# Attention on pairs of 64-row matmuls: three terms for z by z, and sums of each row half in banks of their own

## The chip, the core and the metric

The kernel runs on one core of a Trainium2 chip. The metric is device time in microseconds (us) of one execution. The kernel before was timed in three runs, with a median of 1893.45 us (1893.43 to 1894.5). A profile is one further execution, recorded by the hardware. Engines are named as in the profile: PE is TensorE (PEld its weight loads), DVE VectorE, ACT ScalarE, POOL GpSimd, SP SyncE. A PSUM bank holds 512 float32 columns on 128 partitions (rows); there are eight, `banks[:, 0]` to `banks[:, 7]`.

## The reference

Two stages, with no softmax between them:

```python
# u, v: (4, 3008, 256)   z: (4, 3008, 64)
scores = (1.0 / S) * np.matmul(z, z.transpose(0, 2, 1))   # S = 3008
attn = np.maximum(scores, 0.0) ** 2
out = np.matmul(attn, v)
x = (u * out).reshape(12032, 256)
gate = 1.0 / (1.0 + np.exp(-(x @ w_gate)))                # w_gate, w_val: 256 x 1536
val = x @ w_val
result = gate * val @ w_out                               # w_out: 1536 x 256
```

The change concerns the first stage: the scores (z by z, over 64 elements) and their product with v (over 3008 keys).

## The kernel before

**Precision.** Each float32 operand is split into a high part, rounded by ACT or DVE to the type fp32r, and a low part, the remainder, so a product is a sum of terms: high by high, low by high, high by low.

**Work.** The four batches b are cut into six chunks c of 512 queries (the last has 448) and twelve blocks i of 256 keys, in two halves j of 128 keys each. A step is one (b, c, i): 288 steps, in the order of the list `steps` (line 144). Since the scores are symmetric, a block that an earlier chunk has computed is turned by DVE (`turn`, line 415), stored to DRAM and loaded back later as one of this chunk's steps (`load_back`, line 451): such a step computes no scores (`back`, line 147). One step of each of the first five chunks, the last in its chunk, computes half of its queries (`half`), except in the very first chunk, whose scores are all computed.

**One step.** `pe_scores` (line 334) writes 128 keys by up to 512 queries for each j, into one of two pairs of banks (0 and 1, or 2 and 3) in turn. z has 64 elements a token, and the arrays that hold its parts carry them twice: on rows 0 to 63 and again on 64 to 127. The query tile (`z_query`) holds the high part on the upper 64 rows and the low part on the lower, so one 128-row matmul gives the key part against both query parts: two matmuls for each j, four a step. ACT takes the scores through relu and square into `r` (lines 356, 357), rounds them into `ah` (line 372; on some steps DVE does, line 370), and DVE takes the remainder `al` (line 377). `pe_pv` (line 481) then multiplies by v: for each j and each half d of v's 256 columns, high v by high a, low v by high a, high v by low a. That is twelve 128-row matmuls a step (ten where the last key block is stacked), summed over the chunk's twelve steps in a pair of banks (4 and 5, or 6 and 7, by turns from chunk to chunk), one bank for each d. At a chunk's end `keep` (line 507) copies the two banks to SBUF by one ACT instruction, and a step later sends them to DRAM.

**Order.** The program is written out by hand, in the order in which each engine runs it. In round g of the main loop (line 851) PE gets the scores of step g + 2 and, last, the product of step g. In between stand the loads of later steps, the store and turn of earlier ones, the square, rounding and remainder of step g + 2, jobs entered by round in the tables `before` and `after` (splitting weights, loading z and v of the next batch), and in the first round of a chunk `keep` of the chunk before, behind the rounding. In `after` stand the two DMAs of `z_both` (line 272), which fill the query tile of each chunk ten rounds ahead on SP's queue.

**The end of attention.** The products of the last two steps are issued between the first matmuls of the second stage, by the generator `others` (line 935), in the parts that `pe_pv` yields. That stage uses banks 0 to 3 for its products and 4 to 7 for its sums, and is not part of the change.

Of the kernel before, what the change touches and what calls it, by code (L numbers as in the profile page):

```python
# [9 lines left out]
F32R = mybir.dt.float32r  # L10
# [3 lines left out]
AF = mybir.ActivationFunctionType  # L14
ALU = mybir.AluOpType
# [11 lines left out]
def kernel(  # L27
# [10 lines left out]
    nc = tc.nc  # L38
    P = 128
    B, S, D = u.shape  # L40
# [3 lines left out]
    CH = 512  # L44
    NCH = (S + CH - 1) // CH
    NPAIR = (S + 255) // 256
    NB = D // P
# [21 lines left out]
    v_a, z_a, zq_a, r_a, ah_a, al_a, al2_a, turned_a, raw_a, zt_a, keep_a, w_a, spare_a = map(area, sizes)  # L69
# [9 lines left out]
    banks = ps.tile([P, 8, CH], F32, name="banks")  # L79

    def part(a, kb, cols, dt=F32):

        ap = a[:, int(kb * KB) : int(kb * KB) + cols]
        return ap if dt is F32 else ap.bitcast(dt)

    def f32(ap):
        return ap.bitcast(F32)

    def moving(ap):

        return ap.rearrange("p (t n) -> p n t", t=2)

    def product(ap):

        return ap.rearrange("p (n t) -> p t n", t=2)

    def products(ap):
        return ap.rearrange("p j (n t) -> p j t n", t=2)

    def by_half(ap):  # L100
        return ap.rearrange("p (t n) -> p t n", t=2)

    def by_halves(ap):
        return ap.rearrange("p j (t n) -> p j t n", t=2)
# [39 lines left out]
    steps = [(b, c, i) for b in range(B) for c in range(NCH) for i in order(b, c)]  # L144
    number = {s: g for g, s in enumerate(steps)}
# [93 lines left out]
    z_raw, z_t = {}, {}  # L239

    def z_place(b, p):
        n = (b * NCH + p) % 7
        return part(z_a, 2 * n, CH, F32R), part(z_a, 14 + 2 * n, CH, F32R)

    def z_query(b, p):
        return part(zq_a, 2 * ((b * NCH + p) % 2), CH, F32R)

    def load_z(b, p):
        t = part(w_a, 2 * p, CH) if b == 0 else part(raw_a, 6, CH)
        t = t.rearrange("p (T d) -> p T d", d=32)  # L250
# [17 lines left out]
    def z_low(b, p):  # L268
        hi, lo = z_place(b, p)
        nc.vector.tensor_tensor(lo, z_t[b, p], f32(hi), op=ALU.subtract)  # L270

    def z_both(b, p):
        (hi, lo), q = z_place(b, p), z_query(b, p)
        nc.sync.dma_start(f32(q[0:64]), f32(hi[0:64]))
        nc.sync.dma_start(f32(q[64:128]), f32(lo[64:128]))

# [47 lines left out]
    def keys_of(i, ap, j):  # L326
        if i == NPAIR - 1:
            return ap[:, j * P : j * P + P]
        return ap.rearrange("p (n j) -> p j n", j=2)[:, j]

    sc_t = {}
    counts = {"sc": 0, "turned": 0}

    def pe_scores(s):
        b, c, i = s
        if back(s):
            return
        n = chunk(c)
        k = 2 * (counts["sc"] % 2)
        counts["sc"] += 1  # L340
        sc = banks[:, k : k + 2]
        kh, kl = z_place(b, i // 2)
        q0 = CH // 2 if half(s) else 0
        q = moving(z_query(b, c)[:, q0:n])
        for j in range(2):
            o = (i % 2) * 256
            h, l = (keys_of(i, ap[:, o : o + 256], j) for ap in (kh, kl))
            nc.tensor.matmul(sc[:, j, 0 : n - q0], h, q, start=True, stop=False)  # L348
            nc.tensor.matmul(sc[:, j, 0 : n - q0], l, q, start=False, stop=True)  # L349
        sc_t[s] = sc  # L350

    def square(s):
# [98 lines left out]
    def load_back(s):  # L451
        b, c, i = s
        r = r_of(s)
        if half(s):
            nc.sync.dma_start(r[:, :, 0 : CH // 2], half_t[b, c].rearrange("(p j) q -> p j q", j=2))
        if back(s):
            n, d = chunk(c), shared_t[b, i // 2, c]
            if late(b, i // 2):
                for g in range(4):
                    t = as_stored(i)[32 * g : 32 * g + 32].rearrange("p (I B q) -> p I B q", I=2, q=64)  # L460
                    q0 = 256 * (i % 2) + 64 * g
                    for I in range(2):
                        src = d[I].rearrange("p g j q -> p (g j) q")[:, :, q0 : q0 + 64]
                        nc.gpsimd.dma_start(t[:, I], src)
            else:
                rows = d[256 * (i % 2) : 256 * (i % 2) + 256].rearrange("(p j) q -> p j q", j=2)
                nc.sync.dma_start(r[:, :, 0:n], rows[:, :, 0:n])
# [6 lines left out]
            for k in range(2):  # L474
                nc.vector.transpose(out=dst[:, k], in_=src[:, k])

    def acc_of(b, c):
        k = 4 + 2 * ((b * NCH + c) % 2)
        return banks[:, k : k + 2]

    def pe_pv(s):

        b, c, i = s
        n, k = chunk(c), number[s] % NPAIR
        acc = acc_of(b, c)
        (ah, al), (vh, vl) = a_of(s), v_place(b, i)
        for j in range(2):
            stacked = i == NPAIR - 1 and j == 1
            stop = k == NPAIR - 1 and j == 1
            for d in range(NB):  # L490
                ds = slice(d * P, (d + 1) * P)
                o = acc[:, d, 0:n]
                nc.tensor.matmul(o, vh[:, j, ds], moving(ah[:, j, 0:n]), start=(k == 0 and j == 0), stop=False)  # L493
                if not stacked:
                    nc.tensor.matmul(o, vl[:, j, ds], moving(ah[:, j, 0:n]), start=False, stop=False)  # L495
                if d == 0:
                    yield
            for d in range(NB):
                ds = slice(d * P, (d + 1) * P)
                nc.tensor.matmul(acc[:, d, 0:n], vh[:, j, ds], moving(al[:, j, 0:n]), start=False, stop=stop)  # L500
            yield

# [2 lines left out]
    def keep(b, c, store):  # L507
        n, t0 = chunk(c), b * S + c * CH
        C = b * NCH + c
        if C == B * NCH - 1:  # L510
            t = part(turned_a, 8, 2 * CH)
        else:
            t = part(keep_a, 4 * ((C + 1) % 2) if b < B - 1 else 0, 2 * CH)
        t = t.rearrange("p (h q) -> p h q", h=NB)
        if store:
            nc.sync.dma_start(sums[:, :, t0 : t0 + n], t[:, :, 0:n])
        else:
            nc.scalar.activation(by_halves(t[:, :, 0:n]), products(acc_of(b, c)[:, :, 0:n]), AF.Copy)

# [214 lines left out]
    with tc.manual_schedule():  # L736
# [3 lines left out]
        before, after = {}, {}  # L740

        def at(when, g, f, *args):
            when.setdefault(g, []).append((f, args))
# [6 lines left out]
        for b in range(1, B):  # L750
# [12 lines left out]
            for i in range(NPAIR):  # L763
# [1 line left out]
                at(after, g - 1, load_v, b, i)  # L765
                at(before, g + 2, v_high, b, i)
                at(before, g + 2, v_low, b, i)
        for b in range(B):
            for p in range(NCH):
                if (b, p) != (0, 0):  # L770
                    at(after, b * per + NPAIR * p - 10, z_both, b, p)
        starts = [24, 31, *range(84, 127, 7), *range(156, 199, 7), 246, 261]
        for n, g in enumerate(starts):
            job = Narrow(n)
# [28 lines left out]

        def keep_warm(n):
            for _ in range(n):
                nc.tensor.matmul(banks[:, 7], idle[:, 0:P], idle, start=True, stop=True)

        load_z(0, 0)
        zero = part(r_a, 12, P)
# [6 lines left out]
        load_z(0, 3)  # L816
        turn_z(0, 0)
        z_high(0, 0)
        q = z_query(0, 0)
        nc.scalar.activation(q[0:64], z_t[0, 0][0:64], AF.Copy)  # L820
        z_low(0, 0)
        nc.vector.tensor_copy(q[64:128], f32(z_place(0, 0)[1][64:128]))  # L822
        load_z(0, 4)
        load_v(0, 2)
        keep_warm(11)
# [25 lines left out]
        for g, (b, c, i) in enumerate(steps[:-2]):  # L851
            nxt = steps[g + 2]
            k = g % NPAIR
            early = g < NPAIR
            if g < 3:
                for _ in pe_pv(steps[g]):
                    pass
            pe_scores(nxt)
            if early:
                if k + 2 < NPAIR:  # L860
                    v_low(0, k + 2)
                if k + 5 < NPAIR:
                    load_v(0, k + 5)
                if k in (2, 3, 5):
                    z_low(0, {2: 3, 3: 4, 5: 5}[k])
                if k in (0, 2, 4):
                    turn_z(0, k // 2 + 3)
            for s in steps[g + 5 : g + 8]:
                if number[s] - g == (7 if comes_late(s) else 5):
                    load_back(s)  # L870
            if k == 1 and g > 1:
                keep(*steps[g - 2][:2], True)
            store_turned(steps[g])
            turn(steps[g + 1])
            if not back(nxt):
                square(nxt)
            round_up(nxt)
            rest(nxt)
            if g + 4 < len(steps):
                turn_late(steps[g + 4])  # L880
            run(before, g)
            if early and k + 3 < NPAIR:
                v_high(0, k + 3)
            if early and k in (1, 2, 4):
                z_high(0, {1: 3, 2: 4, 4: 5}[k])
            if k == 0 and g:
                keep(*steps[g - 1][:2], False)
            run(after, g)
            if g >= 3:
                for _ in pe_pv(steps[g]):  # L890
                    pass
# [154 lines left out]
```

## Time and profile before

| what | value |
|---|---|
| median of three timed runs | 1893.45 us (1893.43 to 1894.5) |
| profiled execution, first to last instruction (span) | 1891.7 us |
| PE busy, matmuls | 1880.6 us (99%), 8890 |
| PEld busy, weight loads | 1656.5 us (88%), 8890 |
| DVE busy | 1538.2 us (81%) |
| ACT busy | 1138.8 us (60%) |
| POOL busy | 920.3 us (49%) |

The page gives of the profiled execution the span alone; the 1.75 us between it and the median lie around the first and last instruction or between executions. Matmuls are pipelined and their ends are modelled: a matmul of 512 columns is shown with 379 ns although the next one starts earlier, so strides are read from starts, not from durations. A weight load is shown with some 190 ns beside the matmul before it. In the stretches of rows further down, the columns give each engine's busy time, in brackets its instructions, then the granted clock of PE as a share and the mean busy share of the 16 DMA engines.

### The profile page before, as it was taken

Reading aid. Unit: us, or ns where it says so; the run is one execution under the profiler, and the core shown is the slowest. Engines: PE = TensorE matmul, PEld = TensorE weight load, DVE = VectorE, ACT = ScalarE, POOL = GpSimd, SP = SyncE. Lnnn points to the kernel's source line nnn. Section 1 sums busy time; section 2 is a strip of 40 time slices with the busy share of each in tenths; the row PEclk is TensorE's granted clock in tenths of the full one; section 3 lists DMA queues with packets and bytes.
Section 4 is the critical chain, followed back from the end, with each engine's and each line's share of the span. In section 5 each row is a group of like instructions: output and inputs, shape, how many; then the busy total and the mean of one; then the engine's idle time right before and its main releaser. Section 6 shows DMA issues by size and latency. Waiting matters only on the chain.

```text
span 1891.7 us, 26376 instructions
## 1 busy us (share of the span) xinstructions
PE 1880.6 (99%) x8890; PEld 1656.5 (88%) x8890; DVE 1538.2 (81%) x1957; ACT 1138.8 (60%) x1497; POOL 920.3 (49%) x853
## 2 busy tenths in 40 slices
PE   9999999999999999999999999999999999999998
PEld 7888988889888988889888888888888888888898
DVE  7797688888888786767879787888879797888876
ACT  8886788867887787774444453444444444445443
POOL 4334201230013200003777776877777787778675
PEclk9999999999999999999999999999999999999999
DMA  7789688997799888886542524243342525242331
GB/s 203 182 222 247 184 177 228 276 306 182 177 266 285 249 196 216 220 253 211 173 117 68 145 81 104 84 120 99 90 113 86 126 84 121 81 118 80 99 101 37
DMA packets 552295, 302.98 MB, mean 160 GB/s; under 512 B 490080, under 2 KB 506912, under 8 KB 552160
## 3 DMA queue, kind: packets, MB, share of 16 engines
q1 hardware_dynamic: 534928, 254.51, 51.0%
q0 software_dynamic: 14832, 46.38, 7.8%
q8 instruction: 70, 1.15, 0.3%
q10 hardware_dynamic: 2400, 0.41, 0.1%
q14 instruction: 65, 0.53, 0.1%
HBM read 192.02 MB, written 103.15 MB: 156 GB/s over the span
## 4 chain that ended last, share of the span: by engine, by line
PE 92%; DVE 2%; ACT 2%; DMA 2%; issue 1%; SPq 1%; DVEq 0%; POOL 0%; POOLq 0%
PE banks L693 19%; PE banks L633 12%; PE banks L635 11%; PE banks L634 11%; PE banks L500 11%; PE banks L493 11%; PE banks L495 10%; PE banks L349 3%; PE banks L348 3%; DVE al L377 1%; PE banks L724 1%; DMA shared<-spare 1%; ACT r L356 1%; ACT ah L372 1%; ACT r L357 1%
## 5 line engine op out<-in xcount | busy, mean ns | idle before, releaser
L666 POOL TENSOR_TENSOR keep<-keep,spare 128x512 f32<-128x512 f32 (+1 forms) x284 | 386.6, 1372 | 240.8 <-DVE keep L658 240.8
L377 DVE TENSOR_TENSOR al<-r,ah 128x1024 fp32r<-128x1024 f32 (+1 forms) x287 | 341.0, 1191 | 157.5 <-ACT ah L372 152.0
L493 PE MATMUL banks<-ah,v 128*128 128x512 f32 (+1 forms) x1152 | 428.2, 375 | 0.8 <-DVE ah L385 0.3
L495 PE MATMUL banks<-ah,v 128*128 128x512 f32 (+1 forms) x1104 | 413.5, 375 | 0.0
L500 PE MATMUL banks<-al,v 128*128 128x512 f32 (+1 forms) x1152 | 339.2, 376 | 2.9 <-DVE al L377 2.0
L372 ACT ACTIVATE ah<-r 128x1024 fp32r<-128x1024 f32 (+1 forms) x252 | 256.7, 1034 | 57.1 <-DMA r<-shared 27.4
L670 ACT ACTIVATE h<-keep 128x512 fp32r<-128x512 f32 (+1 forms) x144 | 89.7, 623 | 283.2 <-POOL keep L666 280.1
L658 DVE TENSOR_TENSOR zt<-banks,zt 128x512 f32<-128x512 f32 (+1 forms) x288 | 193.7, 672 | 68.0 <-ACT zt L652 55.5
L500 PEld LDWEIGHTS banks<-al,v 128*128 128x128 f32 x1152 | 216.3, 189 | 33.6 <-DVE al L377 8.3
L493 PEld LDWEIGHTS banks<-ah,v 128*128 128x128 f32 x1152 | 217.7, 189 | 27.4 <-ACT ah L372 1.1
L495 PEld LDWEIGHTS banks<-ah,v 128*128 128x128 f32 x1104 | 208.7, 189 | 24.4
L356 ACT ACTIVATE r<-banks 128x1024 f32<-128x1024 f32 (+2 forms) x169 | 163.1, 965 | 100.1 <-PE banks L349 99.1
L676 POOL TENSOR_TENSOR h<-keep,h 128x512 fp32r<-128x512 f32 (+1 forms) x143 | 187.4, 1311 | 55.7 <-ACT h L670 55.7
L662 ACT ACTIVATE spare<-spare 128x512 f32<-128x512 f32 (+1 forms) x288 | 174.3, 618 | 66.0 <-DVE spare L658 64.5
L658 DVE TENSOR_TENSOR spare<-banks,zt 128x512 f32<-128x512 f32 (+1 forms) x288 | 188.1, 673 | 22.3 <-PE banks L635 21.6
L357 ACT ACTIVATE r<-r 128x1024 f32<-128x1024 f32 (+2 forms) x169 | 170.0, 1006 | 5.4
L652 ACT ACTIVATE zt<-banks 128x512 f32<-128x512 f32 (+1 forms) x144 | 84.0, 583 | 145.3 <-PE banks L635 139.3
L231 POOL DMA_DIRECT2D w_gv<-w x24 | 13.4, 560 | 312.5 <-ACT w L225 299.6
L633 PE MATMUL banks<-z,v 128*128 128x512 f32 x378 | 144.3, 382 | 0.0
L635 PE MATMUL banks<-z,v 128*128 128x512 f32 x378 | 143.3, 379 | 0.0
L348 PE MATMUL banks<-zq,z 128*128 128x512 f32 (+2 forms) x340 | 123.7, 366 | 0.8 <-DVE zq L822 0.8
L670 ACT ACTIVATE v<-keep 128x512 fp32r<-128x512 f32 (+1 forms) x144 | 89.0, 618 | 58.3 <-POOL keep L666 49.2
(161 smaller groups left out, 3930.7 us busy)
## 6 DMA issues: line engine op xcount, KB each, us to landing
v<-w_gv SPq DMA_DIRECT2D x75, 896.0 KB, 4.7
r<-shared SPq DMA_DIRECT2D x72, 512.0 KB, 4.8
shared<-turned SPq DMA_DIRECT2D x236, 128.0 KB, 3.1
r<-shared SPq DMA_DIRECT2D x38, 448.0 KB, 6.0
shared<-spare SPq DMA_DIRECT2D x128, 128.0 KB, 3.4
out_dram<-turned SPq DMA_DIRECT2D x176, 64.0 KB, 2.0
w_gv<-w POOLq DMA_DIRECT2D x24, 448.0 KB, 4.9
sums<-keep SPq DMA_DIRECT2D x20, 512.0 KB, 3.9
```

The costliest lines, as they stand in the source:

```text
L357: nc.scalar.activation(r[:, :, q0:n], r[:, :, q0:n], AF.Square)
L372: nc.scalar.activation(ah[:, :, 0:n], r[:, :, 0:n], AF.Copy)
L377: nc.vector.tensor_tensor(al[:, :, 0:n], r[:, :, 0:n], f32(ah[:, :, 0:n]), op=ALU.subtract)
L493: nc.tensor.matmul(o, vh[:, j, ds], moving(ah[:, j, 0:n]), start=(k == 0 and j == 0), stop=False)
L495: nc.tensor.matmul(o, vl[:, j, ds], moving(ah[:, j, 0:n]), start=False, stop=False)
L500: nc.tensor.matmul(acc[:, d, 0:n], vh[:, j, ds], moving(al[:, j, 0:n]), start=False, stop=stop)
L633: nc.tensor.matmul(o, wt[:, 0, w], xh, start=True, stop=False)
L634: nc.tensor.matmul(o, wt[:, 0, w], xl, start=False, stop=False)
L635: nc.tensor.matmul(o, wt[:, 1, w], xh, start=False, stop=True)
L658: nc.vector.tensor_tensor(to[:, 0:m], bank(J, value, name), s_t[other][:, 0:m], op=ALU.add)
L666: (nc.vector if J == last else nc.gpsimd).tensor_tensor(y, y, g, op=ALU.mult)
L693: nc.tensor.matmul(o, wt[:, half_w, f, ds], moving(ap[:, 0:m]), start=start, stop=stop)
```

## The change

Scores are computed by matmuls on 64 rows: half j = 0 of the keys on rows 0 to 63, j = 1 on rows 64 to 127, each into its own bank, with three terms (high by high, low by high, high by low) and the terms of the two halves taking turns. The query tile goes, with the DMAs and copies that filled it: queries are read from the arrays of z. In the product with v every 128-row matmul becomes two of 64 rows, r = 0 and 1, one after the other in the program; each d now has a pair of banks, one for each r. The order within a step is d, then j, then the three passes. The last two steps of attention keep 128-row matmuls (`whole`), all into the bank of r = 0. `keep` adds the two banks of each d: ACT copies the first, DVE adds the second. It now stands ahead of the stores, the turn and the squares of its round.

Banks 2 to 7 form three pairs that rotate: chunk number C has its sums of d in pair 2C + d, modulo 3. Scores of even steps go to banks 0 and 1, of odd steps to the third pair, which the chunk does not use.

```diff
@@ z_query, and z_both: gone @@
@@ pe_scores @@
+    def rows_half(r):
+        return slice(64 * r, 64 * r + 64)
+    def pair_of_banks(n):
+        k = 2 + 2 * (n % 3)
+        return banks[:, k : k + 2]
+    def scores_of(s):
+        g = number[s] - 2
+        if g % 2:
+            return pair_of_banks(2 * (max(g, 0) // NPAIR) + 2)
+        return banks[:, 0:2]
...
-        k = 2 * (counts["sc"] % 2)
-        counts["sc"] += 1
-        sc = banks[:, k : k + 2]
-        kh, kl = z_place(b, i // 2)
+        sc = scores_of(s)
         q0 = CH // 2 if half(s) else 0
-        q = moving(z_query(b, c)[:, q0:n])
-        for j in range(2):
-            o = (i % 2) * 256
-            h, l = (keys_of(i, ap[:, o : o + 256], j) for ap in (kh, kl))
-            nc.tensor.matmul(sc[:, j, 0 : n - q0], h, q, start=True, stop=False)
-            nc.tensor.matmul(sc[:, j, 0 : n - q0], l, q, start=False, stop=True)
+        o = (i % 2) * 256
+        keys = [ap[:, o : o + 256] for ap in z_place(b, i // 2)]
+        queries = [moving(ap[:, q0:n]) for ap in z_place(b, c)]
+        for x, (kx, qx) in enumerate(((0, 0), (1, 0), (0, 1))):
+            for j in range(2):
+                r = rows_half(j)
+                nc.tensor.matmul(
+                    sc[:, j, 0 : n - q0], keys_of(i, keys[kx], j)[r], queries[qx][r], start=x == 0, stop=x == 2
+                )
@@ pe_pv @@
-    def acc_of(b, c):
-        k = 4 + 2 * ((b * NCH + c) % 2)
-        return banks[:, k : k + 2]
+    def acc_of(b, c, d):
+        return pair_of_banks(2 * (b * NCH + c) + d)
...
+        whole = number[s] >= len(steps) - 2
+        for d in range(NB):
+            acc = acc_of(b, c, d)
+            ds = slice(d * P, (d + 1) * P)
+            for j in range(2):
+                passes = [(vh, ah), (vl, ah), (vh, al)]
+                if i == NPAIR - 1 and j == 1:
+                    del passes[1]
+                for x, (vx, ax) in enumerate(passes):
+                    start = k == 0 and j == 0 and x == 0
+                    ends = j == 1 and x == len(passes) - 1
+                    halves = [(0, slice(0, P))] if whole else [(r, rows_half(r)) for r in range(2)]
+                    for r, p in halves:
+                        stop = ends and number[s] in ((len(steps) - 1, len(steps) - 3)[r], number[s] - k + NPAIR - 1)
+                        nc.tensor.matmul(acc[:, r, 0:n], vx[p, j, ds], moving(ax[p, j, 0:n]), start=start, stop=stop)
+                yield
@@ keep @@
-            nc.scalar.activation(by_halves(t[:, :, 0:n]), products(acc_of(b, c)[:, :, 0:n]), AF.Copy)
+        for d in range(NB):
+            to, acc = by_half(t[:, d, 0:n]), acc_of(b, c, d)
+            nc.scalar.activation(to, product(acc[:, 0, 0:n]), AF.Copy)
+            nc.vector.tensor_tensor(to, product(acc[:, 1, 0:n]), to, op=ALU.add)
@@ main loop, round g @@
+            if k == 0 and g:
+                keep(*steps[g - 1][:2], False)
             if k == 1 and g > 1:
                 keep(*steps[g - 2][:2], True)
             store_turned(steps[g])
...
-            if k == 0 and g:
-                keep(*steps[g - 1][:2], False)
             run(after, g)
```

Beside these, the matmuls that keep PE's clock up before the first scores write bank 5 and not 7.

## Rows read from the trace of the kernel before

**Rows 1.** The page's totals: busy us, share of the span, instructions.
```profile
span 1891.7 us, 26376 instructions
...
PE 1880.6 (99%) x8890; PEld 1656.5 (88%) x8890; DVE 1538.2 (81%) x1957; ACT 1138.8 (60%) x1497; POOL 920.3 (49%) x853
```

**Rows 2.** The chain of waits that ended last, by engine.
```profile
PE 92%; DVE 2%; ACT 2%; DMA 2%; issue 1%; SPq 1%; DVEq 0%; POOL 0%; POOLq 0%
```

**Rows 3.** Timeline of PE at a chunk's end: start us, us, engine, line, operation.
```profile
265.18 0.38 PE L348 MATMUL banks<-zq,z 128*128 128x512 f32 x1
...
272.08 0.38 PE L348 MATMUL banks<-zq,z 128*128 128x512 f32 x1
```

**Rows 4.** The same in a chunk of 448 queries.
```profile
207.00 0.35 PE L348 MATMUL banks<-zq,z 128*128 128x448 f32 x1
...
208.51 0.54 PE L500 MATMUL banks<-al,v 128*128 128x448 f32 x2
```

**Rows 5.** Groups of PE's matmuls by line and shape: count, busy us, mean ns, idle before.
```profile
L493 PE MATMUL banks<-ah,v 128*128 128x512 f32 x960 | 361.2, 380 | 0.8 <-DVE ah L385 0.3 <-DVE ah L370 0.2 <-ACT ah L372 0.2
L495 PE MATMUL banks<-ah,v 128*128 128x512 f32 x920 | 348.7, 379 | 0.0
...
L348 PE MATMUL banks<-zq,z 128*128 128x512 f32 x282 | 107.0, 379 | 0.8 <-DVE zq L822 0.8
...
L493 PE MATMUL banks<-ah,v 128*128 128x448 f32 x192 | 67.0, 352 | 0.0
L495 PE MATMUL banks<-ah,v 128*128 128x448 f32 x184 | 64.9, 352 | 0.0
...
L348 PE MATMUL banks<-zq,z 128*128 128x256 f32 x38 | 9.7, 277 | 0.0
L348 PE MATMUL banks<-zq,z 128*128 128x448 f32 x20 | 7.1, 353 | 0.0
```

**Rows 6.** Timeline of PE and its loads where a step has 256 queries.
```profile
259.10 0.27 PE L348 MATMUL banks<-zq,z 128*128 128x256 f32 x1
259.10 0.19 PEld L349 LDWEIGHTS banks<-zq,z 128*128 128x128 f32 x1
...
259.22 0.20 PEld L348 LDWEIGHTS banks<-zq,z 128*128 128x128 f32 x1
...
259.34 0.20 PEld L349 LDWEIGHTS banks<-zq,z 128*128 128x128 f32 x1
...
259.56 0.38 PE L493 MATMUL banks<-ah,v 128*128 128x512 f32 x1
```

**Rows 7.** Timeline in the first steps, where PE had waited: two loads, two matmuls.
```profile
10.80 0.30 PEld L500 LDWEIGHTS banks<-al,v 128*128 128x128 f32 x2 [0.48 <-DVE al L390]
10.80 0.70 PE L500 MATMUL banks<-al,v 128*128 128x512 f32 x2
```

**Rows 8.** Timeline of PE at the kernel's end, nine matmuls of 256 columns.
```profile
1880.91 1.17 PE L724 MATMUL banks<-al,v 128*128 128x256 f32 x9
```

**Rows 9.** The page's groups of instructions: reads of a bank by DVE and ACT.
```profile
L658 DVE TENSOR_TENSOR zt<-banks,zt 128x512 f32<-128x512 f32 (+1 forms) x288 | 193.7, 672 | 68.0 <-ACT zt L652 55.5
...
L652 ACT ACTIVATE zt<-banks 128x512 f32<-128x512 f32 (+1 forms) x144 | 84.0, 583 | 145.3 <-PE banks L635 139.3
```

**Rows 10.** Timeline of ACT and DVE at the chunk's end of rows 3.
```profile
271.85 1.06 ACT L372 ACTIVATE ah<-r 128x1024 fp32r<-128x1024 f32 x1
...
272.94 1.23 DVE L377 TENSOR_TENSOR al<-r,ah 128x1024 fp32r<-128x1024 f32 x1 [0.71 <-ACT ah L372]
```

**Rows 11.** Timeline of ACT before the first scores are squared.
```profile
6.71 0.63 ACT L301 ACTIVATE v<-turned 128x512 fp32r<-128x512 f32 x1 [0.85 <-DMA turned<-in_v_dram]
```

**Rows 12.** Stretches of chunks (b, c) = (0, 0), (1, 4) and (2, 2), columns as told above.
```profile
12.40:55.60 43.20, 42.76 (x194) 36.34 (x193) 33.97 (x44) 37.82 (x45) 21.66 (x40) 1.00 0.66 190
...
384.00:415.30 31.30, 30.55 (x142) 25.95 (x141) 26.15 (x35) 22.51 (x25) 12.56 (x21) 1.00 0.96 299
...
526.80:563.60 36.80, 36.80 (x174) 32.47 (x173) 31.95 (x38) 32.67 (x35) 7.33 (x12) 1.00 1.02 261
```

More of the change, by code (lines that the diff above doesn't have):

```diff
@@ L243, in z_place @@
         return part(z_a, 2 * n, CH, F32R), part(z_a, 14 + 2 * n, CH, F32R)
-    def z_query(b, p):
-        return part(zq_a, 2 * ((b * NCH + p) % 2), CH, F32R)
     def load_z(b, p):
@@ L270, in z_low @@
         nc.vector.tensor_tensor(lo, z_t[b, p], f32(hi), op=ALU.subtract)
[L272 to L275, printed above, removed]
     v_raw = {}
@@ L331 @@
     sc_t = {}
-    counts = {"sc": 0, "turned": 0}
+    counts = {"turned": 0}
+    def rows_half(r):
[8 more added lines that the diff above has]
+        return banks[:, 0:2]
     def pe_scores(s):
@@ L484, in pe_pv @@
         n, k = chunk(c), number[s] % NPAIR
-        acc = acc_of(b, c)
         (ah, al), (vh, vl) = a_of(s), v_place(b, i)
[L487 to L501, printed above, removed]
+        whole = number[s] >= len(steps) - 2
[14 more added lines that the diff above has]
+                yield
     sums = dram.tile([P, NB, N], F32, name="sums")
@@ L516, in keep @@
             nc.sync.dma_start(sums[:, :, t0 : t0 + n], t[:, :, 0:n])
-        else:
-            nc.scalar.activation(by_halves(t[:, :, 0:n]), products(acc_of(b, c)[:, :, 0:n]), AF.Copy)
+            return
+        for d in range(NB):
+            to, acc = by_half(t[:, d, 0:n]), acc_of(b, c, d)
+            nc.scalar.activation(to, product(acc[:, 0, 0:n]), AF.Copy)
+            nc.vector.tensor_tensor(to, product(acc[:, 1, 0:n]), to, op=ALU.add)
     groups = [(t0, min(CH, (N - t0) // 2)) for t0 in range(0, N, 2 * CH)]
@@ L767 @@
                 at(before, g + 2, v_low, b, i)
[L768 to L771, printed above, removed]
         starts = [24, 31, *range(84, 127, 7), *range(156, 199, 7), 246, 261]
@@ L805, in keep_warm @@
             for _ in range(n):
-                nc.tensor.matmul(banks[:, 7], idle[:, 0:P], idle, start=True, stop=True)
+                nc.tensor.matmul(banks[:, 5], idle[:, 0:P], idle, start=True, stop=True)
         load_z(0, 0)
@@ L818 @@
         z_high(0, 0)
-        q = z_query(0, 0)
-        nc.scalar.activation(q[0:64], z_t[0, 0][0:64], AF.Copy)
         z_low(0, 0)
-        nc.vector.tensor_copy(q[64:128], f32(z_place(0, 0)[1][64:128]))
         load_z(0, 4)
```

## The prediction

> **What bounds the kernel now.** I read the page's totals first: PE is busy for 1880.6 us of a span of 1891.7 [rows 1]. A busy PE need not be PE at its peak, so next I read the chain of waits: it runs through PE for 92% [rows 2]. Last I looked at where matmuls start. In attention, 32 matmuls of 512 columns lie between 265.18 and 272.08 us, one every 6.90/32 = 0.2156 us [rows 3]; at 448 columns eight take 1.51 us, 0.189 each [rows 4]. The time goes with the columns and nothing lies between. So PE is bound by columns, and what counts is how many slots of 0.2156 us there are. The load of each matmul's weights runs beside the matmul before it, hidden.
>
> **What changes in slots.** Differences are worked out in the profiled execution (span 1891.7 us) and put on the median of the timed runs, 1893.45, which lies 1.75 us above that span.
>
> Scores. Line 348 has 282 matmuls of 512 columns, 20 of 448 and 38 of 256, two for each step, so 141, 10 and 19 steps compute scores; line 349 has as many again [rows 5]. Each of these steps has four 128-row matmuls: for j = 0 and 1, high keys and low keys, each against high and low queries stacked on 128 rows. After, it has three terms for each j on 64 rows, j = 0 on rows 0 to 63 and j = 1 on 64 to 127: six matmuls, three slots if two of them run side by side. Four of 256 columns now take 0.46 us, 0.115 each [rows 6]. One slot less a step is 141 x 0.2156 + 10 x 0.189 + 19 x 0.115 = 30.4 + 1.9 + 2.2 = 34.5 us.
>
> Product with v. Lines 493, 495 and 500 have 960 + 920 + 960 = 2840 matmuls of 512 columns and 192 + 184 + 192 = 568 of 448 (line 500 counts as line 493) [rows 5]. The last two steps (24 of the latter) stay on 128 rows. The other 3384 become pairs: each half has the same columns, so a pair costs one slot if the halves run together. The trace has no 64-row matmul, so its cost is open between two ends. Side by side: 0. One behind the other: 2840 x 0.2156 + 544 x 0.189 = 715 us more. I take 0: the halves share neither rows nor a bank, and in the rows PE is a stream of columns through rows.
>
> Weight loads. Each half has a load of its own, of 128 columns as before. Two loads on end take 0.30 us [rows 7] where one takes 0.19 [rows 6], so the second starts 0.11 after the first; their two matmuls span 0.70, of which 0.38 is the second one [rows 7] and 0.2156 a stride, which leaves 0.104 for the same load. I take 0.108 a load. Two of them make 0.216 us, almost exactly a slot of 512 columns: were loads to follow one another, they would just hide there, and not under 448 or 256 columns. If besides a load waits until the matmul before it has started, the rows of 256 columns give the step: loads 0.12 apart, each starting with a matmul, 0.117 a matmul for the keys ((259.56 - 259.10 - 0.11)/3) [rows 6], and (1.17 - 0.27)/8 = 0.1125 for nine with other weights [rows 8]. Halves that load beside each other show none of this: 0, the end that I take, as each half has rows of its own.
>
> The Trainium skill bears on this twice (TensorE: Matmul & The Clock Gate). "LDWEIGHTS (loading the stationary operand)" says that a load's time goes by its columns, so that one of few rows costs as much as a full one; by that rule halving the rows halves no load, which speaks against the change, and rivals 1 and 2 are what it would do here. Part 3, "The mechanism" and "What overlaps and what doesn't", says that loads overlap matmuls in flight when their row groups differ, and that tiles start about 4 ns apart; if each of the 3894 pairs paid those 4 ns, an estimate from the page is 15.6 us more and the sum would be -4 us. No row of before shows either.
>
> **The handover at a chunk's end.** Before, two pairs of banks for sums alternate, and ACT copies one at leisure (line 518, behind the rounding). After, three pairs rotate. The d = 1 sums of a new chunk go into the pair that held the old chunk's d = 0 sums, so PE waits for an ACT copy of 128x512 out of a bank (583 ns in line 652) and then a DVE add out of a bank (672 ns in line 658) [rows 9]. Their place in the queues decides. Take the boundary at 272.08, where the old chunk's matmuls end [rows 3]. ACT is at line 372 from 271.85 for 1.06 us; the copy follows at 272.9 and ends at 273.5. DVE starts the remainder, line 377, at 272.94 for 1.23 us, to 274.17 [rows 10]; the add ends at 274.85. PE does three slots of scores (0.65) and six of d = 0 (1.29) and is ready for d = 1 at 272.08 + 1.94 = 274.02. It stands for about 0.85 us. This needs two computed steps in a row, as at the boundaries into chunks 0, 1 and 2 of a batch, 11 of 23; where the second is loaded back, the rounding is over earlier and I count up to 0.1. That is 11 x 0.85 + 1 = 10 us more. The ends are 0 (the add in time everywhere) and 23 x 1.7 = 39 (every boundary, each with twice the delay). Behind the waiting copy on ACT stand the second copy and the next squares; behind the add on DVE the next turn and remainder, which PE's own stop gives time.
>
> **What is taken away or moved.** 46 copies of z into the query tile leave SP's queue: a relief, counted 0. The two small ones at the start go; PE waits 0.8 us for the second [rows 5], but ACT stands until 6.71 for v's transfer anyway [rows 11], so I take 0, with -0.8 as the end. Since ACT and not PE paces the first steps, the slots of some four steps there are saved in vain: 1 us more. The low part of a is wanted at the third slot of a step and not the fifth, 0.43 us earlier: by rows 10 it is there at 274.17, for a step that starts at 272.08 + 0.65 + 2.59 + 0.65 = 275.97, so 0; up to 1 us a chunk if that cover goes, within the 39 above.
>
> **What the DMAs give back.** In chunks 2 to 4 of batches 1 and 2 the DMA engines are busy for 0.96 to 1.02 of the time, and PE stands 31.30 - 30.55 = 0.75 us in one of these six stages [rows 12]. There, and in the same three of batch 3, the change saves 18 slots a batch, 11.6 us in all. I take a third of it, 4 us, as lost to late loads; the ends are 0 and 11.6. In the first chunk ACT is busy for 37.8 of 43.2 us [rows 12], which stays under the 40.6 that are left after twelve slots: 0.
>
> **Sum.** -34.5 + 0 + 10 + 1 + 4 = -19.5 us: 1874 us, 1.0% faster. With the ends of the last terms this case reaches from 1862 to 1886, and beyond that it is rival 4.
>
> **The rivals.**
> 1. *Loads in one line, without gaps.* Slots of 0.216: product 2840 x 0.0004 + 544 x 0.027 = 15.8 more; scores 510 x 0.216 = 110.2 in place of 137.9 (141 x 0.862 + 10 x 0.756 + 19 x 0.46), 27.7 less; with 10 and 1 for the rest 1893. For it: even with PE idle two loads are 0.108 apart [rows 7]. Against: those were loads into the same rows.
> 2. *Each load also waits for the start of the matmul before it.* Slots of 0.225 and 0.234: product 2840 x 0.0094 + 544 x 0.036 = 46.3 more; scores 510 x 0.234 = 119.3, 18.6 less; with 10 at chunk ends 1931. This is the side slower than before; it decides from a slot of 0.2162, where 3894 slots and the 11 us of the rest come to the 853 us (612.3 + 102.8 + 137.9) that the same work takes now. For it: each load in rows 6 starts with a matmul. Against: there the same rows are loaded and in use, which explains it as well.
> 3. *The halves don't run together*, so the change doesn't do what it says: 715 more for the product, and for scores two slots more in place of one less, 141 x 0.431 + 10 x 0.378 + 19 x 0.23 = 69 more: about 2680. For it: no row shows two matmuls at once. Against it no row speaks either.
> 4. *The handover eats the gain.* At 1.7 us for each of 23 boundaries: 1893.45 - 34.5 + 39 + 4 = 1902; it decides from 1.3 us a boundary. For it: DVE's own work ahead of the add. Against: half the boundaries have a loaded step, and slack.
>
> **How the numbers follow.** The forecast has 0.45, the rivals 0.15, 0.18, 0.10 and 0.12. A change below 0.2%, 3.8 us, can't be told from none here. Faster: 0.43 of the forecast, 0.05 of rival 1 and 0.02 of rival 4, so 0.50. The same: 0.01, 0.07 and 0.03, so 0.11. Slower: the rest, 0.39. The range 1860 to 1935 leaves out rival 3 and the outer part of the forecast and of rival 2, about 0.17 in all. The likeliest case by itself has 1862 to 1886.
>
> **What will show it.** In the new trace, pairs of score and product matmuls should start 0.2156 us apart from pair to pair at 512 columns and 0.189 at 448: 0.216 at both is rival 1, 0.225 rival 2, 0.43 rival 3. A computed step should shrink from 16 slots (3.45 us) to 15 (3.23). The new DVE add should release PE at 11 boundaries after some 0.85 us of idle time, and ACT's waits for loaded steps should grow in chunks 2 to 4. The prediction is wrong if a pair is longer than its columns, or if PE stands much over 1 us at a boundary.

## The result, and the profile after

The changed kernel takes 1921.53 us (median of four runs, 1918.37 to 1922.55) against 1893.55 for the kernel before on the same chip: a ratio of 1.0139 on record, 95% interval 1.0125 to 1.0154. It is slower by 28 us, where 19.5 us less was forecast. The time lies inside the range, on the other side of the forecast.

The page of the changed kernel: totals, then the groups of the product with v (line 507) and of the scores (line 354).

```profile
span 1919.5 us, 33838 instructions
...
PE 1868.9 (97%) x12614; PEld 1638.3 (85%) x12614; DVE 1563.3 (81%) x2004; ACT 1140.3 (59%) x1520; POOL 921.4 (48%) x853
...
L507 PE MATMUL banks<-ah,v 64*128 64x512 f32 (+1 forms) x4496 | 748.1, 376 | 39.2 <-DVE keep L528 31.4
...
L507 PE MATMUL banks<-al,v 64*128 64x512 f32 (+1 forms) x2296 | 621.4, 377 | 4.7 <-DVE al L384 3.6
...
L354 PE MATMUL banks<-z 64*128 64x512 f32 (+2 forms) x1020 | 162.8, 370 | 0.0
```

PE is busy 11.7 us less than in [rows 1], in a span that is 27.8 longer. What [rows 5] had nowhere is the idle time before line 507, put down to line 528: the DVE add at a chunk's end.

A timeline of the changed kernel across the boundary into chunk (2, 0), all engines:

```profile
457.15 0.72 PE L507 MATMUL banks<-ah,v 64*128 64x448 f32 x4
...
457.53 0.53 PE L507 MATMUL banks<-al,v 64*128 64x448 f32 x2
...
459.30 0.89 DVE L429 STREAM_TRANSPOSE spare<-r 128x512 f32<-128x512 f32 x1
...
460.02 0.71 DVE L377 CAST ah<-r 128x1024 fp32r<-128x1024 f32 x1
460.06 0.78 PE L507 MATMUL banks<-ah,v 64*128 64x512 f32 x4
460.07 0.96 ACT L527 ACTIVATE keep<-banks 128x448 f32<-128x448 f32 x2
...
460.50 0.56 PE L507 MATMUL banks<-al,v 64*128 64x512 f32 x2
...
460.83 1.23 DVE L384 TENSOR_TENSOR al<-r,ah 128x1024 fp32r<-128x1024 f32 x1
...
461.36 0.38 PE L507 MATMUL banks<-ah,v 64*128 64x512 f32 x1
...
461.98 0.42 DVE L301 TENSOR_TENSOR v<-raw,v 128x256 fp32r<-128x256 f32 x1
462.42 0.42 DVE L303 TENSOR_TENSOR v<-raw,v 64x256 fp32r<-64x256 f32 x1
462.88 1.16 DVE L528 TENSOR_TENSOR keep<-banks,keep 128x448 f32<-128x448 f32 x2
...
463.56 0.70 PE L507 MATMUL banks<-ah,v 64*128 64x512 f32 x3 [1.82 <-DVE keep L528]
```

Two things are to be seen. First, a pair costs one slot: the four matmuls at 457.15 are two pairs, and the next start 0.38 later, 0.19 a pair of 448 columns; from 460.06 to 460.50 two pairs of 512 columns take 0.44, the slot of [rows 3]. Second, ACT's copies are done by 461.03, before the old chunk's banks are wanted. DVE has in front of the add half a turn (429), a rounding (377), a remainder (384) and two pieces of v's low part (301, 303), and comes to it at 462.88. PE, whose last matmul before the wait starts at 461.36, could go on a slot later, at about 461.6, and stands until 463.56.

The waits of PE, then of its loads, for the whole execution: waiting line, releaser, us in total, times, longest.

```profile
PE banks L507 <- DVE keep L528: 31.4, 22, 2.7
PE banks L507 <- ACT keep L527: 7.0, 5, 3.6
```

```profile
PEld banks L507 <- DVE keep L528: 38.8, 22, 3.1
PEld banks L507 <- DVE al L384: 11.0, 20, 1.3
PEld banks L507 <- ACT keep L527: 10.0, 8, 4.0
```

At the boundary into chunk (1, 1), which the prediction prices at 0.85 us:

```profile
277.65 0.70 PE L507 MATMUL banks<-ah,v 64*128 64x512 f32 x3 [0.90 <-DVE keep L528]
```

Stretches of the changed kernel; columns as in [rows 12], the granted clock third from the right:

```profile
117.30:120.70 3.40, 3.40 (x38) 3.11 (x36) 3.40 (x4) 3.13 (x5) 1.81 (x3) 1.00 0.84 239
...
133.45:136.62 3.17, 3.17 (x19) 2.47 (x17) 1.11 (x2) 3.04 (x3) 0.00 (x0) 0.50 0.44 165
171.00:174.40 3.40, 2.93 (x14) 2.40 (x16) 2.75 (x4) 0.00 (x0) 0.98 (x2) 0.50 0.78 247
...
806.60:810.00 3.40, 3.40 (x32) 3.00 (x34) 3.33 (x7) 1.69 (x2) 0.00 (x0) 1.00 1.02 233
```

The second follows a stand of PE at a boundary and the third begins in the last half microsecond of one: PE runs at 1.2 GHz there, half of what the first shows. The trace has seven such stretches in attention, each from within a stand or from just after it. But not every stand of that length has one: the fourth stretch follows the longest wait for DVE's add, 2.7 us, at full clock. Over the execution the mean granted clock is 0.994, against 0.999 before; (0.999 - 0.994) x 1919.5 is some 9.6 us. The loads' standing of 38.8 + 10.0 us and these 9.6 make 58, of the 62.5 that lie between the slots saved (-34.5) and the result (+28). That is a rough sum: by the idle time of PE itself the same waits are 31.4 + 7.0 = 38.4 us, and what they cost lies between the two, since a load stands before its matmul does and a matmul's end is modelled.

How long some chunks took, from the first start of a chunk's products to that of the next, worked out from the starts in the traces (us), and the slots in that time (matmuls, or pairs, at 0.2157, 0.189 and 0.112 us by columns):

```
chunk        slots            took
             before  after    before   after   e1_act_release   e6_low_last   e12_half_loads
(0, 0)       41.85   39.04    43.97    42.52   42.59            42.33         41.94
(0, 3)       34.53   33.55    34.70    40.23   39.78            39.66         40.48
(1, 0)       40.57   38.08    40.61    40.21   38.12            38.12         38.12
(1, 2)       37.12   35.50    37.16    39.95   36.71            36.95         36.94
(1, 3)       34.53   33.55    35.53    38.73   37.77            37.29         37.32
(1, 4)       33.56   32.83    35.15    38.28   35.92            35.10         35.12
all but the last (23)
             829.1   795.1    838.1    864.9   833.8            829.7         825.2
```

So 34.0 us of slots went in these chunks, as forecast; what lies above the slots rose from 9.0 to 69.8. (The profiled execution of e6_low_last took 1885.35 us, the longest of its four.)

### The profile page after: what moved, and what is told of

Same layout as the page of the kernel before. It is cut to its first block, busy times and chain, and to the rows that moved or that the text cites. A ratio compares the mean times of both kernels' runs of the same rounds, so it can differ in the third digit from the quotient of the medians.

```text
span 1919.5 us, 33838 instructions
## 1 busy us (share of the span) xinstructions
PE 1868.9 (97%) x12614; PEld 1638.3 (85%) x12614; DVE 1563.3 (81%) x2004; ACT 1140.3 (59%) x1520; POOL 921.4 (48%) x853
## 4 chain that ended last, share of the span: by engine, by line
PE 70%; DVE 2%; ACT 2%; issue 1%; DMA 1%; SPq 0%; DVEq 0%; POOL 0%; POOLq 0%
PE banks L703 18%; PE banks L507 15%; PE banks L643 11%; PE banks L644 11%; PE banks L645 11%; PE banks L354 2%; ACT ah L379 1%; ACT r L363 1%; ACT r L364 1%; PE banks L734 1%; DVE al L384 1%; DMA shared<-turned 1%; DVE keep L528 0%; DVE turned L433 0%; DVE spare L433 0%
## 5 line engine op out<-in xcount | busy, mean ns | idle before, releaser
L507 PE MATMUL banks<-ah,v 64*128 64x512 f32 (+1 forms) x4496 | 748.1, 376 | 39.2 <-DVE keep L528 31.4
L507 PEld LDWEIGHTS banks<-ah,v 64*128 64x128 f32 x4496 | 598.8, 188 | 98.2 <-DVE keep L528 38.8
L507 PE MATMUL banks<-al,v 64*128 64x512 f32 (+1 forms) x2296 | 621.4, 377 | 4.7 <-DVE al L384 3.6
L507 PEld LDWEIGHTS banks<-al,v 64*128 64x128 f32 x2296 | 387.9, 188 | 37.5 <-DVE al L384 11.0
L354 PE MATMUL banks<-z 64*128 64x512 f32 (+2 forms) x1020 | 162.8, 370 | 0.0
L354 PEld LDWEIGHTS banks<-z 64*128 64x128 f32 x1020 | 126.5, 196 | 10.6 <-ACT z L263 0.8
L668 DVE TENSOR_TENSOR keep<-banks,spare 128x512 f32<-128x512 f32 (+1 forms) x144 | 97.3, 676 | 32.2 <-PE banks L645 28.7
```

The source lines that it names most:

```text
L354: nc.tensor.matmul(sc[:, j, 0 : n - q0], keys_of(i, keys[kx], j)[r], queries[qx][r], start=x == 0, stop=x == 2)
L507: nc.tensor.matmul(acc[:, r, 0:n], vx[p, j, ds], moving(ax[p, j, 0:n]), start=start, stop=stop)
L668: nc.vector.tensor_tensor(to[:, 0:m], bank(J, value, name), s_t[other][:, 0:m], op=ALU.add)
```

## The experiments

Theory 1: PE stands at chunk ends for the release of banks through DVE's queue, and the clock falls after long stands. Theory 2: pairs of 64 rows are dear in themselves. Theory 3: late DMA loads set the pace. Ratios are to the kernel before, as on record, with 95% intervals; the quotients of the medians come out up to 0.1% higher. In the code, "..." marks lines left out.

**e1_act_release.** ACT empties both banks of each d, DVE adds later from SBUF. The second copy goes to the old query tile's place, so an operand of the second stage that lay there moves to a tile of its own (left out below).

```diff
             nc.scalar.activation(to, product(acc[:, 0, 0:n]), AF.Copy)
-            nc.vector.tensor_tensor(to, product(acc[:, 1, 0:n]), to, op=ALU.add)
+            if C == B * NCH - 1:
+                nc.vector.tensor_tensor(to, product(acc[:, 1, 0:n]), to, op=ALU.add)
+            else:
+                nc.scalar.activation(by_half(part(zq_a, 2 * d, n)), product(acc[:, 1, 0:n]), AF.Copy)
+        if C < B * NCH - 1:
+            for d in range(NB):
+                nc.vector.tensor_tensor(t[:, d, 0:n], part(zq_a, 2 * d, n), t[:, d, 0:n], op=ALU.add)
...
```

> Changed kernel, but at a chunk's end ACT copies both banks of each d (the second into the old query tile's place) and DVE adds the copies later, from SBUF; only the last chunk keeps the DVE add out of the bank. Theory 1 (the loss is PE standing for DVE's add, which queues behind other DVE work, and the slower clock after long stands): PE's idle time for DVE at line 528, 31 us, goes; ACT's four copies of some 0.5 us come in its stead, so 10 to 15 us of standing are left and fewer half-clock stretches: 1875 to 1886 us. Theory 2 (64-row pairs themselves are dear, by loads, issue or clock): 1915 to 1925, little changed. Theory 3 (late DMA loads set the pace): within 5 us of 1921.

1888.67 us, 0.9961 (0.9947 to 0.9975): 33 us less than the changed kernel, and faster than before. DVE does the same 46 adds (678 ns each in place of 675), only not in front of PE; ACT does two more copies a chunk. Waits of PE's loads in this kernel, where no line of the old kind is left for DVE's add:

```profile
PEld banks L507 <- DVE al L384: 25.6, 41, 1.3
PEld banks L507 <- ACT keep L527: 10.0, 8, 4.0
...
PEld banks L507 <- ACT zq L531: 4.0, 14, 0.3
```

The time is 3 us above theory 1's bounds: of the freed time, some 15 us went to the loads' wait for the low part of a (line 384), 25.6 here and 11.0 in the changed kernel.

**e4_no_add.** The second half's sums are left out.

```diff
-            nc.vector.tensor_tensor(to, product(acc[:, 1, 0:n]), to, op=ALU.add)
```

> Changed kernel without the DVE add at a chunk's end: the sums of the lower row half are left out of the output, and the banks of r = 1 are never read. Theory 1: PE's idle time for line 528 (31 us, 39 for its loads) is gone with no work in its stead, some of the half-clock stretches too; the waits for ACT's copies (7 to 10 us) stay: 1870 to 1885 us. Theory 2 or 3: 1915 or more.

1882.79 us, 0.9934 (0.9914 to 0.9954), as theory 1 has it; theories 2 and 3 fall as the main cause.

**e5_keep_late.** The copies and adds back behind the remainder, where the kernel before had its copy.

```diff
-            if k == 0 and g:
-                keep(*steps[g - 1][:2], False)
             if k == 1 and g > 1:
...
+            if k == 0 and g:
+                keep(*steps[g - 1][:2], False)
             run(after, g)
```

> Changed kernel with the copy and add put back at their old place in the round, behind the turn, the rounding and the remainder of step g + 2. Theory 1: DVE reaches the add later by a turn (1.5 us where there is one) and a remainder (1.2), and the remainder now also waits for the next scores: 2 to 4 us more at each of 23 boundaries, 1965 to 2010 us, with more half-clock stretches. Theory 2 or 3: 1915 to 1930.

2005.79 us, 1.0583 (1.0562 to 1.0605), as theory 1 has it: 84 us more than the changed kernel, by order in the queues alone. PE's waits and the clock in this kernel:

```profile
PE banks L507 <- ACT keep L527: 46.5, 22, 3.7
PE banks L507 <- DVE keep L528: 36.1, 23, 3.3
```

```profile
core 0: 2003.6 us, clock 0.973
```

(1 - 0.973) x 2003.6 is 54 us of clock, as against (1 - 0.994) x 1919.5 = 11.5: the fall of the clock is a large part of what long stands cost here, though some of the 54 falls into the standing itself.

**e2_scores_alone.** The kernel before with the change's scores alone (product and banks as before).

```diff
-        for j in range(2):
...
+        for x, (kx, qx) in enumerate(((0, 0), (1, 0), (0, 1))):
+            for j in range(2):
+                r = slice(64 * j, 64 * j + 64)
+                key = keys_of(i, (kh, kl)[kx][:, o : o + 256], j)
+                nc.tensor.matmul(sc[:, j, 0 : n - q0], key[r], queries[qx][r], start=x == 0, stop=x == 2)
```

> Kernel before, with only the scores in 64-row pairs (three terms, no query tile); the product with v, its banks and the copy at a chunk's end are those of before, on 128 rows, so PE changes between 64 and 128 rows twice in each of 170 computed steps. Theory 1, if changing costs nothing: one slot less a step and no handover, 1893.5 - 34.5 + 1 = 1860 us. If each change waits until the array has run empty (a matmul of 512 columns is shown with 379 ns at a stride of 216, so some 0.16 us each), 340 changes cost 55 us: 1915. Theory 2 (pairs are dear): over 1893 as well, with pairs of scores longer than 0.216 us.

1923.17 us, 1.0148 (1.0132 to 1.0163). Timeline of PE and its loads over one computed step of this kernel:

```profile
300.34 0.48 PE L486 MATMUL banks<-ah,v 128*128 128x512 f32 x1
...
303.13 0.51 PEld L342 LDWEIGHTS banks<-z 64*128 64x128 f32 x6 [0.33 <-issue]
303.13 0.92 PE L342 MATMUL banks<-z 64*128 64x512 f32 x6
...
303.97 0.19 PEld L486 LDWEIGHTS banks<-ah,v 128*128 128x128 f32 x1 [0.33 <-issue]
303.97 0.48 PE L486 MATMUL banks<-ah,v 128*128 128x512 f32 x1
```

From the first product matmul of a step to that of the next are 3.63 us, where fifteen slots are 3.23: a change between 128 and 64 rows costs 0.2 us, two a step. The whole time agrees: 1923.17 is 62.8 us over 1894.89 - 34.5 (1894.89 is the kernel before beside this run), 0.18 for each of 340 changes. Loads stop at each change: none runs beside the last matmul of the other kind. So the saving of scores by itself is lost, and the product's move to pairs, which saves no slot, is what lets it pay in e1 and e6. The Trainium skill (TensorEngine Tiling (Array Packing), "Key Properties") says that changing the tiling mode drains the engine; this trace agrees, at 0.2 us each.

**e6_low_last.** On e1: within each d the high passes of both j first, then the two low ones.

```diff
...
+            passes = [(j, vx, ax) for group in ([(vh, ah), (vl, ah)], [(vh, al)]) for j in range(2) for vx, ax in group]
...
```

> Release by ACT (e1_act_release) with one more edit: within each d the two high passes of both j come first and the two of the low part last, so the low part of a is wanted at the fifth slot of a step, as in the kernel before, and not at the third. Theory: the 9.9 us that PE stands for line 384 in e1_act_release (25.6 for its loads) come from that order; most of it goes: 1888.7 - 8 to 10 = 1879 to 1882 us. Rival: DVE is late by more than two slots at those places, then it gives back 1 to 3 us only.

1881.99 us, 0.9929 (0.9912 to 0.9945): 6.7 less than e1. The wait for line 384 at PE falls from 9.9 to 5.2 us. The time is at the upper end of theory's bounds; the gain, 6.7, lies between theory (8 to 10) and rival (1 to 3): half of the wait was this order. In its trace 34.6 us still lie above the slots, as against 9.0 before.

**e8_first_batch.** On e6, another place for the first batch's sums. At the boundary into chunk (0, 3), the longest stand of the changed kernel, its timeline reads:

```profile
128.03 0.38 PE L507 MATMUL banks<-al,v 64*128 64x512 f32 x2
...
130.03 1.29 DVE L482 STREAM_TRANSPOSE r<-keep 128x512 f32<-128x512 f32 x2
...
131.40 1.09 ACT L527 ACTIVATE keep<-banks 128x512 f32<-128x512 f32 x2 [4.54 <-issue]
...
132.05 0.48 PE L507 MATMUL banks<-ah,v 64*128 64x512 f32 x1 [3.65 <-ACT keep L527]
```

ACT's copy goes into the keep tile, from which DVE still turns a late block (line 482, over at 131.32).

```diff
+            t = part(zq_a, 0, 2 * CH) if b == 0 else part(keep_a, 4 * ((C + 1) % 2) if b < B - 1 else 0, 2 * CH)
...
+        if b == 0:
+            for d in range(NB):
+                nc.scalar.activation(by_half(t[:, d, 0:n]), product(acc_of(b, c, d)[:, 0, 0:n]), AF.Copy)
+                if d == 0:
+                    nc.scalar.activation(by_half(part(spare_a, 8, n)), product(acc_of(b, c, d)[:, 1, 0:n]), AF.Copy)
+            to = by_half(t[:, 1, 0:n])
+            nc.vector.tensor_tensor(to, product(acc_of(b, c, 1)[:, 1, 0:n]), to, op=ALU.add)
...
```

> e6_low_last with the sums of the first batch kept in the old query tile's place and a free part of the spare tile, so that ACT's copies no longer wait until DVE has turned the late blocks that lie in the keep tile. Theory: the 6.9 to 10 us of standing for ACT's copy, of which 4.4 lie at one boundary of the first batch, go: 4 to 8 us less than e6_low_last, 1872 to 1877 us. Rival: the next wait takes their place there (the add out of the bank for d = 1 is on DVE again): no more than 2 us.

1882.93 us, 0.9940 (0.9925 to 0.9955): no gain over e6. Chunk (0, 3) fell from 39.66 to 36.77 us in its trace, but the next one rose from 33.76 to 35.05. There PE stands for the DVE add out of the bank (line 530 of this kernel), as the rival has it:

```profile
PE banks L354 <- DVE zq L530: 2.4, 2, 1.9
```

**e10_four_terms.** On e1, a fourth pair in each step.

```diff
-        for x, (kx, qx) in enumerate(((0, 0), (1, 0), (0, 1))):
+        for x, (kx, qx) in enumerate(((0, 0), (1, 0), (0, 1), (1, 1))):
...
```

> Release by ACT with a fourth term, low keys by low queries, in each computed step: eight 64-row matmuls, four pairs, as many slots as the four 128-row matmuls of before. Theory: a pair costs its columns, so 141 x 0.2156 + 10 x 0.189 + 19 x 0.112 = 34.4 us come back: 1923 us, less what the longer step hides of the waits left (up to 10): 1913 to 1923. Rival (the third term's saving is not what e1_act_release gained): within 10 us of 1889.

1908.72 us: 20 more than e1, between theory and rival, 4 below the theory's bounds. Of 34.4 us of slots some 13 were taken out of a wait, that for the low part (25.6 in e1):

```profile
PEld banks L507 <- DVE al L384: 12.4, 23, 1.2
```

So the third term's saving is real, and in e1 two fifths of it went into waiting.

**e11_halves_apart.** On e1, three passes of the upper half, then three of the lower.

```diff
...
+                for r, p in [(0, slice(0, P))] if whole else [(r, rows_half(r)) for r in range(2)]:
+                    for x, (vx, ax) in enumerate(passes):
...
```

> Release by ACT with the product's order changed: for each d and j the three passes of rows 0 to 63 come first, then the three of rows 64 to 127. If PE starts matmuls in program order and two overlap only when neighbours use different halves, one pair in three is left beside: four slots where three were, 2840 x 0.0719 + 544 x 0.063 = 238 us more, about 2127. If PE reached further ahead in its queue for the free half, 1889. If nothing overlapped here, 2600.

1895.80 us: 7 more than e1, not 238. Program order across halves does not bind. In its timeline of PE, the scores of rows 0 to 63 run beside the last product passes of rows 64 to 127, though the program has all of these first:

```profile
302.37 0.38 PE L506 MATMUL banks<-al,v 64*128 64x512 f32 x2
302.59 0.38 PE L354 MATMUL banks<-z 64*128 64x512 f32 x1
302.59 0.38 PE L506 MATMUL banks<-ah,v 64*128 64x512 f32 x1
302.81 0.38 PE L354 MATMUL banks<-z 64*128 64x512 f32 x1
302.81 0.38 PE L506 MATMUL banks<-al,v 64*128 64x512 f32 x1
```

**e12_half_loads** and **e13_add_on_pool**, on e6, for what is left.

```diff
-                nc.sync.dma_start(r[:, :, 0:n], rows[:, :, 0:n])
+                nc.sync.dma_start(r[:, :, 0 : n // 2], rows[:, :, 0 : n // 2])
```

> e6_low_last with every loaded-back block loaded by half (each row's first half of the queries; the second half keeps what an earlier step left there, so that part of the output is left out). Theory A (what is left above the slots in chunks 2 to 4, some 9 to 13 us over batches 1 and 2, is late loads on DMA engines busy over 0.93 of the time): the DMA share falls to 0.8 or less there, chunk 3 of batches 1 and 2 falls from 37.3 and 39.0 us to near its slots' 34.3, and the kernel gives 1868 to 1874 us. Theory B (DVE, busy for 33.9 of 37.3 us in that chunk, sets its pace): chunk 3 stays over 36.5 us, 1879 to 1883.

1880.73 us, 1.3 less than e6; chunk (1, 3) stays at 37.32. The same stretch of e6_low_last, then of this run (the mean share of the DMA engines second from the right):

```profile
340.90:378.20 37.30, 35.41 (x318) 29.54 (x318) 33.88 (x41) 30.97 (x37) 10.28 (x17) 1.00 0.97 267
...
340.90:378.20 37.30, 35.38 (x318) 29.52 (x318) 33.95 (x41) 30.94 (x37) 10.22 (x17) 1.00 0.79 216
```

The DMA engines are relieved, and ACT's waits for loaded blocks there, 2.5 us in e6, are gone; the chunk is no shorter. Theory 3 (A in the expectation) falls for the rest too. Chunk (2, 3) did fall, from 38.98 to 36.40 us, but it took 36.53 in e14_keep_before_jobs, which loads whole blocks, so that is not put down to the loads.

```diff
-                nc.vector.tensor_tensor(t[:, d, 0:n], part(zq_a, 2 * d, n), t[:, d, 0:n], op=ALU.add)
+                nc.gpsimd.tensor_tensor(t[:, d, 0:n], part(zq_a, 2 * d, n), t[:, d, 0:n], op=ALU.add)
```

> e6_low_last with the two adds of the copies at a chunk's end on POOL in place of DVE (1.3 us of DVE a chunk less; POOL's own queue gets two adds of some 1.4 us). Theory B: the chunks 1 to 4, where DVE is busiest, give back 0.5 to 1.3 us each: 1868 to 1876 us. Theory A: 1880 to 1883, unchanged; or a little more if loads of v and z, issued by POOL behind the adds, come later.

1895.37 us, 13 more. Chunk (1, 3) is 37.38: with the adds off DVE it is no shorter. The adds wait on POOL for ACT's copies,

```profile
POOL keep L533 <- ACT zq L530: 291.9, 21, 34.9
```

and the DMA issues behind them wait too. The last chunks of batches 0 to 2 took 32.7 to 34.0 us in place of 29.4 to 30.5; that late loads of v, which POOL issues there, are the reason was not tried.

**e14_keep_before_jobs** and **e15_both.** At the boundary into chunk (1, 4), e6's timeline shows the handover in ACT's queue: its copy stands behind line 225, which had waited 2.0 us for DVE.

```profile
379.35 0.95 ACT L225 ACTIVATE w<-w 128x896 fp32r<-128x896 f32 x1 [2.00 <-DVE w L221]
...
380.21 0.58 ACT L526 ACTIVATE keep<-banks 128x512 f32<-128x512 f32 x1
...
380.84 1.40 PE L505 MATMUL banks<-ah,v 64*128 64x512 f32 x7 [1.21 <-ACT keep L526]
```

```diff
-            if k == 0 and g:
-                keep(*steps[g - 1][:2], False)
...
+            if k == NPAIR - 1:
+                for _ in pe_pv(steps[g]):
+                    pass
+                keep(b, c, False)
             run(before, g)
...
```

> e6_low_last with the product of a chunk's last step issued, and ACT's four copies queued, ahead of the jobs entered for that round (splitting weights, parts of v and z), and not behind them. Theory 1 (what is left at the chunk ends is the same handover, now in ACT's queue: at two boundaries of e6_low_last the copies follow jobs of 0.6 to 0.9 us, or one that itself waits 2.0 us for DVE): PE's standing for ACT's copies, 9.2 us, falls to 4 to 6 (the first batch keeps its wait for the keep tile), and chunk (1, 3) from 37.3 to near 36: 1875 to 1879 us. Rival: ACT now waits in its queue for PE's last sums and the jobs and squares behind it come late: 1882 or more.

> e14_keep_before_jobs with the first batch's sums kept as in e8_first_batch. Theory 1: the two edits act at different boundaries, so their gains add: 1871 to 1877 us. Rival: in the first batch the DVE add out of the bank (d = 1) is a handover through DVE again and takes the gain back: no better than e14_keep_before_jobs.

1883.20 us (0.9943, 0.9928 to 0.9958) and 1882.09 (0.9934, 0.9918 to 0.9951): no better than e6, within the bounds of both rivals. PE's wait for ACT's copies fell from 9.2 to 6.0 us in e14, and the kernel's time did not follow: 1.3 us of waiting for ACT's rounding (line 379) came in its stead, as the rival has it, and chunk (1, 3) stayed at 37.29. What kept the other 2 us from showing is open.

The best of these, e6_low_last, is 0.7% faster than the kernel before.

## Why the prediction was wrong

- *Scores in three slots, pairs for one slot, loads beside each other:* right. Pairs of 512 and 448 columns take 0.22 and 0.19 us; e10 shows that a term costs its slots less what waits give. Rivals 1 to 3 did not happen. In e2, six loads start within 0.51 - 0.19 = 0.32 us, where one line of loads at 0.108 would need 0.54. The Trainium skill (TensorE: Matmul & The Clock Gate, Part 3, "What overlaps and what doesn't") says that loads overlap matmuls in flight only when row groups differ; the loads of the two halves do run beside matmuls here, and beside each other (the "only" isn't borne out: in [rows 6] 128-row loads start beside 128-row matmuls). The 4 ns a pair that I priced by the page cost nothing: chunk (1, 0) of e1 took 38.12 us for 38.08 of slots, where 4 ns for each of its some 175 pairs would add 0.7.
- *The handover:* this step failed. I priced 11 boundaries at 0.85 us and the other 12 at up to 0.1, in all 10 us. The trace has 48.8 us of standing loads over 23 boundaries, 2.1 each (by PE's own idle time 38.4, 1.7 each), which is the mechanism of rival 4 at its price of 1.7 or more. I read DVE's queue at one boundary, into chunk (1, 1), where only a remainder stood before the add, and there the price was right: PE's idle time in the changed kernel is 0.90 us (277.65 above), and 0.85 to 0.90 at the like boundaries of the other batches. But it is over 1 us at 16 of the 23. At others half a turn, a rounding, parts of v and z and the splitting of weights stand there too, since the round before ends with those jobs, as at 461.98 above. (In the kernel before, the old chunk's matmuls end at 268.63, and not a step later at 272.08, as I read it. ACT comes to line 372 there at 268.46 and DVE to 377 at 269.55, so the sum is nearly the same.) And the boundaries that I took for free, into chunks with a loaded second step, are among the worst: (0, 3) took 5.5 us more than before, (1, 3) 3.2 and (1, 4) 3.1. At (0, 3) it was not DVE's add but ACT's copy that came late: it stood for the keep tile until DVE had turned a block out of it (131.32 above), a wait that the prediction does not have.
- *The clock:* left out. No row of before had a stand of PE long enough to show it; some 9.6 us came from stretches at 1.2 GHz in and after stands.
- *The low part of a, wanted two slots earlier, counted 0:* wrong in e1, where the banks no longer came first: the order costs about 5 us at PE (e6). In the changed kernel itself this wait was 3.6 us.
- *What the DMAs give back, 4 us:* not borne out. Chunks 2 to 4 do take more than their slots (in e6 3.7 us in (1, 3)), but half the loaded bytes change nothing there, so it isn't the DMA engines' load. ACT's order at the boundary isn't it either (e14), and taking the adds off DVE gave nothing (e13), though the delays that this brought on POOL could hide a gain. What holds these chunks stays open; DVE, busy for 33.9 of 37.3 us in (1, 3), is not ruled out.
- *The start, 1 us:* of that size: chunk (0, 0) has 2.8 us of slots less and took 1.45 less.
- *The likeliest case's 1862 to 1886:* its own lowest ends (handover 0, small copies -0.8, start 1, DMAs 0) add up to 1859. That the measured time lies inside the wide range is no merit of the forecast: only rivals reach there.

## What to carry to other kernels

When a change takes away spare buffers, price the release of each one by everything that stands before it in the releasing engine's queue, at each place where it happens, and not at one. Let an engine with a short queue empty the bank and do the arithmetic later from SBUF: the same adds cost 33 us less. A long stand of PE can cost more than its length: after seven of them here PE ran at the lower clock.

## What the runs showed that I had not expected

The two row halves of PE run as two streams: with their passes three apart (e11) they still overlap, out of program order, at 7 us for the whole kernel. The Trainium skill (TensorE: Matmul & The Clock Gate, Part 3, "What overlaps and what doesn't") calls matmuls strictly first in, first out; for matmuls on different halves this run differs, and the measurement decides. And a change between 128 and 64 rows costs 0.2 us each way, as much as a slot, so one slot saved between two changes is a loss of one.
